# The last pass of a decode backward kernel: three engines in the written order, or in an order chosen at compile time with only the slab products kept in place

## The chip, the cores and the metric

The kernel runs on one core of one Trainium2 chip. The metric is device time in microseconds (us) of one execution; three executions of the kernel before are given, and their median is the number to compare with. One further record, the profile, shows when each instruction of one execution ran.

## The reference, cut to what matters

A decoder step for one token goes through attention, a dense layer, the same attention again and the same dense layer again, with the same weights and caches both times. The kernel computes the output and all gradients:

```
x = x + A(layernorm(x), k_cache, v_cache, wq, wo)   # 32 query heads, 4 groups, 65536 keys of 128
x = x + B(layernorm(x), w1, b1, w2, b2)             # squared relu, 3584 wide
x = x + A(layernorm(x), ...)
x = x + B(layernorm(x), ...)
out, vjp = jax.vjp(f, x, k_cache, v_cache, wq, wo, w1, b1, w2, b2);  grads = vjp(grad_out)
```

The gradients of the two caches are as large as the caches (67 MB each, bf16), and each is a sum over both attention layers of outer products, so that the last pass reads both caches and writes both gradients.

## The kernel before, in words

There are four passes over the caches: two forward passes, one backward pass for the upper attention layer, and a last pass (`attn_bwd4`) that does the backward of the lower layer and writes the cache gradients of both layers. Dense stages stand between them.

The last pass goes through 256 items, each of 8 columns of 128 keys, in four groups g; four items are a block (J = 32 columns). `pipeline` calls, for each step i, a list of stages, each with a lag in steps; a stage is a Python function that issues instructions for the item that is due:

- `vT` (L1313): loads the block of V when it is new, transposes 8 tiles on TensorE (L1321) into a PSUM tile `ps_tr`, and evicts it into a tile `kt` (four buffers).
- `vS` (L1341): 8 matmuls of `kt` with `DOB` into `ps_sc` (L1352, one buffer in this pass), once a block opened by a matmul at L1349; at the block's end VectorE multiplies with the kept exponentials into `X` (L1369).
- `eIn` (L1327): GpSimd copies a block of exponentials into `xin` (L1330, one buffer). `eT` (L1373) and `xT` (L1379): four transposes a block each (L1336) and an eviction into `xt`. `eT` also sets up small matrices (`su_setup`: L1296 on VectorE, L1301 on GpSimd, L1303 on TensorE, L1305 and L1307 on VectorE).
- `dV8` and `dK8` (`outer16`, L1384): the outer products that are the cache gradients. Each fills a 128x1024 PSUM tile `ps_gg` with a pair of 512-wide matmuls (L1392), which ScalarE or VectorE evicts into a staging slot (L161 and L164, the two lines of the helper `evac`); a full slot is stored from GpSimd's queue (L1398). There are 512 such pairs in the pass and two `ps_gg` buffers.
- `k8` (L1411): 8 matmuls of the K block with `X` into `ps_acc` (L1423).

Beside these, `bg.step` issues one piece of background work in a step: the outer products of the weight gradients (`rows2` L1455 and `rank2` L1470, which also use `ps_gg`), and the products of weight slabs with a vector (`g_rowdots`: VectorE multiplies a slab with the vector at L583, ScalarE sums it at L572). In this pass L583 is already followed by `tc.keep_in_program_order(ins)`, which puts the product behind the instruction of VectorE that was written before it.

The order of the work: the pass stands in `tc.manual_schedule(engines=ORDERED)`, where ORDERED is TensorE, VectorE and ScalarE. In these the instructions stay in the order in which the Python code issues them. SyncE (the loads, L350 for the caches and L447 for the weights) and GpSimd (copies, stores) are not in the set: the framework's list scheduler places their instructions at compile time, by its own estimate of when inputs and buffers are ready, and among ready ones by the written order. Each engine then runs its queue strictly in that order. Loads and stores use slots of one arena that the Python code hands out in the written order.

`evac` chooses between ScalarE and VectorE by running totals of estimated work, while the Python code runs. At the end of the pass, `fill4` (ten steps before the end) transposes the last weight slabs (L669), and after the pass the last gradient rows are computed and stored (L1491, L208).

Of the kernel before, what the change touches and what calls it, by code (L numbers as in the profile page):

```python
# [11 lines left out]
F32 = mybir.dt.float32  # L12
ACTF = mybir.ActivationFunctionType
ALU = mybir.AluOpType
AX = mybir.AxisListType
PSUM = bass.MemoryType.PSUM
P = 128
# [3 lines left out]
def kernel(  # L21
# [24 lines left out]
    nc = tc.nc  # L46
    D = A_x.shape[-1]
# [7 lines left out]
    DC, FC = D // P, F // P  # L55
# [10 lines left out]
    TLEAD = 2  # L66
# [9 lines left out]
    tmp = ctx.enter_context(tc.tile_pool(name="tmp", bufs=2))  # L76
# [23 lines left out]
    def ps_mv(shape, dtype=F32):  # L100
        if PS["pass4"]:
            return ps_tr(shape, dtype)
        return PS["pool"].tile(shape, dtype, name="ps_mv", tag="mv", bufs=1)
# [98 lines left out]
    def col_to_dram(col, n, v1d):  # L202
        nj = n // P
        pt = ps_mv([nj, P], F32)
        nc.tensor.transpose(pt[:, :], col[:, :], ident_f[:, :])
        rows = tmp.tile([nj, P], BF, name="rows_c", tag="rows_c")
        nc.vector.tensor_copy(out=rows[:], in_=pt[:])
        nc.gpsimd.dma_start(out=v1d.rearrange("(j p) -> j p", p=P), in_=rows[:])  # L208

    def bcast_sum(src, ncols, mean=False):  # L210
        pt = ps_mv([P, ncols], F32)
        nc.tensor.matmul(pt[:, :], lhsT=(onesd_f if mean else ones_f)[:, :], rhs=src, start=True, stop=True)
        return pt
# [23 lines left out]
    def ln_bwd(dn, n, rstd):  # L237
        st = tmp.tile([P, 2], F32, name="lnb_st")
        nc.vector.reduce_sum(out=st[:, 0:1], in_=dn, axis=AX.X)
        pr = tmp.tile([P, DC], F32, name="lnb_pr")  # L240
        nc.vector.tensor_tensor(out=pr[:], in0=dn, in1=n[:], op=ALU.mult)
        nc.vector.reduce_sum(out=st[:, 1:2], in_=pr[:], axis=AX.X)
        tot = bcast_sum(st[:], 2, mean=True)
        negm = tmp.tile([P, 2], F32, name="lnb_negm")
        nc.vector.tensor_scalar(out=negm[:], in0=tot[:], scalar1=-1.0, scalar2=None, op0=ALU.mult)
        t = tmp.tile([P, DC], F32, name="lnb_t")
        nc.vector.scalar_tensor_tensor(out=t[:], in0=n[:], scalar=negm[:, 1:2], in1=dn, op0=ALU.mult, op1=ALU.add)
        dx = tmp.tile([P, DC], F32, name="lnb_dx")
        nc.vector.tensor_scalar(out=dx[:], in0=t[:], scalar1=negm[:, 0:1], scalar2=rstd[:, 0:1], op0=ALU.add, op1=ALU.mult)
        return dx  # L250
# [20 lines left out]
    def hold(i):  # L271
        HELD.add(i)
        FREE.pop(i, None)
# [122 lines left out]
    DK_LAG = TLEAD + J // 8 + 1  # L396
    B4_LAG = DK_LAG + J // 8
    DV_LAG = TLEAD + 1
    V_LEAD = 4 * J // 8
    ITEMS = [order_by_unit(False, SU), order_by_unit(True, SU), order_by_unit(False, HB), order_by_unit(True, J)]  # L400
    V_SHIFT = lambda k: min(V_LEAD, max(0, (k - V_LEAD) // 3))
# [197 lines left out]
    class Rows:  # L599
# [147 lines left out]
        def run(self):  # L747
            self.fill()
            first = self.queue[0][0] if self.queue else None
            while first is not None and first["inplace"] and self.queue and self.queue[0][0] is first:  # L750
                self.back()
            self.fill()
            while self.queue:
                self.back()
                self.fill()
# [67 lines left out]
    def tasks(i):  # L823
        for fn in TASKS.pop(i, ()):
            fn()

    def pipeline(items, stages, bg, end=(), holds=(), lead=None):

        def due(lag):
            at = {}  # L830
            for k, it in enumerate(items):
                at.setdefault(k + lag + LEAD if lead is None or lag >= 0 else k + ~lag + lead(k), []).append(it)
            return at
        LEAD = 0 if lead is None else lead(len(items))
        when = [due(l) for _, l in stages]
        maxlag = max(l for _, l in stages) + LEAD
        for i in range(len(items) + maxlag):
            NOW["i"] = i
            NOW["wide"] = NOW["pairs"]
            for at, k in holds:  # L840
                if i == at:
                    hold(k)
            tasks(i - 0.5)
            for n, (fn, lag) in enumerate(stages):
                for it in when[n].get(i, ()):
                    fn(*it)
                if n == 0:
                    tasks(i)
            bg.step(max(0, i - LEAD))
            NOW["wide"] = False  # L850
            NOW["step"] += 1
            for before, fn in end:
                if i == len(items) + maxlag - before:
                    fn()
        while TASKS:
            k = min(TASKS)
            NOW["i"] = int(k + 0.5)
            tasks(k)


    def new_layer(name, lay):
        L = dict(name=name)
        for nm in ("qT", "oT", "rZ", "dOT", "dqT"):
            L[nm] = vec.tile([P, HQ], F32, name=name + "_" + nm)
        L["oTb"] = vec.tile([P, HQ], BF, name=name + "_oTb")
        L["qpad"] = vec.tile([P, G, 8, R], BF, name=name + "_qpad")
        L["negm"] = vec.tile([P, G, NSU, R], F32, name=name + "_negm")
        L["fw"] = vec.tile([P, G, NSU, R], F32, name=name + "_fw")
        L["nd2"] = vec.tile([64, HQ], BF, name=name + "_nd2")
        nc.gpsimd.memset(L["nd2"][:], 0.0)  # L870
        return L
# [22 lines left out]
    def gsl(g):  # L894
        return slice(g * R, (g + 1) * R)
# [81 lines left out]
    def g_dn(L, dn, g, first):  # L977
        yield from g_rowdots(wq_slabs(g)[0], DC, L["dqT"][:, gsl(g)], R, dn_finish(dn, first), "%s_dn%d" % (L["name"], g))
# [4 lines left out]
    ORDERED = {mybir.EngineType.PE, mybir.EngineType.DVE, mybir.EngineType.Activation}  # L983
# [281 lines left out]
    def attn_bwd4(p, La, Lb, on_group, bg, stack, end=()):  # L1265
        dspool = stack.enter_context(tc.tile_pool(name="b4_ds", bufs=2))
        items = ITEMS[p]
# [170 lines left out]
        for b in range(V_LEAD * 8 // J // 2):  # L1438
            nexts.append(("k",) + items[(b + 2) * J // 8])
            nexts.append(("v",) + items[(b + NKEEP[2]) * J // 8])  # L1440
        with tc.manual_schedule(engines=ORDERED):
            pipeline(items, [(eIn, 0), (dV8, DV_LAG), (dK8, DK_LAG), (xT, DK_LAG - 1), (vS, ~TLEAD), (eT, TLEAD), (vT, ~0), (k8, B4_LAG)], bg,
                     end, lead=V_SHIFT)

# [48 lines left out]
    def g_outer(pool, out_dram, nA, nB, a_cols, b_cols, c0=0, a_f=False):  # L1495

        rb = pool.tile([66, 4 * P], BF, name="rowb", tag="rowb")
        rows2(b_cols, (0, 4), rb)
        yield
        for a0 in range(0, nA, 4):  # L1500
            ra = pool.tile([66, 4 * P], BF, name="rowa", tag="rowa", bufs=2)
            rows2(a_cols, (a0, a0), ra)
            yield
            sl = Slot("og", True)
            og = sl.t[:, :].rearrange("p (j n) -> p j n", j=4)
            for j in range(4):
                rank2(og[:, j, :], lambda r: d_cols(ra[r, :], j) if a_f else f_cols(ra[r, :], j), lambda r: rb[r, :])
                if j < 3:
                    yield
            nc.gpsimd.dma_start(out=out_dram[a0 * P:(a0 + 4) * P, c0:c0 + 1024].rearrange("(p j) n -> p j n", j=4), in_=og)  # L1510
            sl.free(stored=True)
            yield
# [39 lines left out]
    L1, L3 = new_layer("L1", 0), new_layer("L3", 1)  # L1552
# [33 lines left out]
    PRE = {}  # L1586

    def pre_load(key, pair):
        def f():
            PRE[key] = prefetch(pair())  # L1590
        return f

    gxbc = bcast_vec(gx[:], DC)
    bg = Background()
# [17 lines left out]
    rows = Rows(DENSE["pool"])  # L1612
# [20 lines left out]
    bg = Background()  # L1633
# [14 lines left out]
    rows = Rows(DENSE["pool"])  # L1648
# [15 lines left out]
    bg = Background()  # L1664
# [15 lines left out]
    dx1 = vec.tile([P, DC], F32, name="dx1")  # L1680
# [12 lines left out]
    rows = Rows(DENSE["pool"])  # L1693
# [27 lines left out]
    bg = Background()  # L1721
# [6 lines left out]
    dn1 = vec.tile([P, DC], F32, name="dn1")  # L1728
# [13 lines left out]
    def gwq(g):  # L1742
        return g_outer(bgpool, out_4, DC, R, [L3["n"], L1["n"]], [L3["dqT"][:, gsl(g)], L1["dqT"][:, gsl(g)]], c0=g * 1024)

    def on4(g):
        if g != lastg[3]:
            bg.add(g_dn(L1, dn1, g, g == firstg[3]))
            bg.normal.append(gwq(g))

    def last_v():  # L1750

        for g, c8 in ITEMS[3][-3 * J // 8::J // 8]:
            kv8("v", g, c8)

    def fill4():
# [5 lines left out]
                                  lastg[3] * 1024)  # L1761
        next(PRE["gwq"])
    attn_bwd4(3, L1, L3, on4, bg, b4, [(12 + B4_LAG, last_v), (20, pre_load("wq4", lambda: wq_slabs(lastg[3], 2))), (10, fill4)])
    next(PRE["gwq"])
    PRE["rows"].run()
    next(PRE["gwq"])
    dxn1 = ln_bwd(dn1[:], L1["n"], L1["rstd"])
    dx0 = tmp.tile([P, DC], F32, name="dx0")
    nc.vector.tensor_tensor(out=dx0[:], in0=dx1[:], in1=dxn1[:], op=ALU.add)
    col_to_dram(dx0, D, out_1.rearrange("a b d -> (a b d)"))  # L1770
    run(PRE["gwq"])
    b4.close()
    ps4_stack.close()

# [29 lines left out]
```

## Time and profile before

| | |
|---|---|
| three runs | 2132.25, 2144.49 (median), 2154.23 us |
| profiled execution, its own time | 2144.49 us |
| its span, first to last instruction | 2142.7 us |
| mean granted TensorE clock | 0.852 of full speed |
| last pass, first matmul of `vS` to last of `k8` | 1212.7 to 2124.5 us |
| moved by DMA over the span | 794.98 MB |

The profiled execution is the median run; 1.8 us of its time lie outside the span. In the views below, PE is TensorE's matmuls, PEld its weight loads, DVE VectorE, ACT ScalarE, POOL GpSimd, SP SyncE (SPq its queue). A line of waits reads: engine, what waited and its line, the releaser, the total, the number of times, the longest.

### The profile page before, as it was taken

What the parts mean: (1) busy time and instruction counts of PE and PEld (TensorE: products, weight loads), DVE (VectorE), ACT (ScalarE), POOL (GpSimd) and SP (SyncE); (2) the same over time, 40 slices, a digit from 0 to 9 for tenths busy, and PEclk for the clock granted to TensorE, in tenths of its full rate; (3) what the DMA queues carried; (4) which work ended last, traced back from release to release, by engine and by line L of the source; (5) the groups of instructions that cost most, each with busy time, mean ns of one, the idle gap of its engine ahead of it and who ended that gap; (6) DMA issues with size and microseconds to landing.
All of it is one profiled execution on the core that took longest, in us unless ns stands there. A gap on an engine that the chain in (4) does not pass through costs nothing. (4 is left out here: it accounts for less than half of the span.)

```text
span 2142.7 us, 67169 instructions
## 1 busy us (share of the span) xinstructions
PE 1657.9 (77%) x30228; PEld 1348.5 (63%) x30228; DVE 1185.3 (55%) x2414; ACT 1047.8 (49%) x1620; POOL 141.7 (7%) x332
## 2 busy tenths in 40 slices
PE   7887776887788878788788777777676777787775
PEld 6877776787777767677778644444454545454443
DVE  5655553464555445354445556656477567656655
ACT  3434443354344534254443456546466556656654
POOL 0000000000000000000000011111011111111111
PEclk9989997899999979998999867758699779869877
DMA  9999999999999989999999769879799979999954
GB/s 393 421 424 420 425 424 391 389 422 423 420 424 424 406 307 367 421 423 412 424 416 361 263 236 375 351 291 368 287 388 387 395 284 405 386 350 370 360 231 177
DMA packets 101038, 794.98 MB, mean 371 GB/s; under 512 B 9472, under 2 KB 9486, under 8 KB 37134
## 3 DMA queue, kind: packets, MB, share of 16 engines
q1 hardware_dynamic: 76670, 624.99, 72.9%
q0 software_dynamic: 24080, 165.70, 18.9%
q8 instruction: 236, 3.87, 0.7%
q14 instruction: 52, 0.43, 0.1%
HBM read 624.96 MB, written 165.69 MB: 369 GB/s over the span
## 5 line engine op out<-in xcount | busy, mean ns | idle before, releaser
L164 DVE COPY kt<-ps_tr 128x1024 bf16<-128x1024 bf16 x715 | 491.2, 688 | 462.2 <-PE ps_tr L1009 252.2
L161 ACT CAST arena<-ps_gg 128x1024 bf16<-128x1024 f32 (+2 forms) x445 | 429.8, 1002 | 262.3 <-PE ps_gg L1470 142.1
L1009 PE MATMUL ps_tr<-ident_b,arena 128*128 128x128 bf16 x3840 | 313.7, 227 | 41.0 <-DMA arena<-in_A_k_cache_dram 28.4
L164 DVE CAST arena<-ps_gg 128x1024 bf16<-128x1024 f32 (+1 forms) x198 | 241.4, 1220 | 166.9 <-PE ps_gg L1392 150.4
L1392 PE MATMUL ps_gg<-GG,xt 64*128 64x512 bf16 x1024 | 227.1, 457 | 134.4 <-ACT arena L161 85.0
L161 ACT COPY kt<-ps_tr 128x1024 bf16<-128x1024 bf16 x173 | 180.5, 1048 | 201.9 <-PE ps_tr L1201 116.7
L1009 PEld LDWEIGHTS <-arena 128*128 128x128 bf16 x3840 | 236.9, 102 | 50.7 <-DMA arena<-in_A_k_cache_dram 32.1
L1111 PE MATMUL ps_acc<-arena 128*128 128x64 bf16 (+4 forms) x4096 | 207.9, 197 | 60.3 <-DMA arena<-in_A_v_cache_dram 48.9
L1392 PEld LDWEIGHTS <-xt 64*128 64x128 bf16 x1024 | 53.2, 97 | 251.6 <-issue 214.8
L1111 PEld LDWEIGHTS <-arena 128*128 128x128 bf16 x4096 | 161.5, 101 | 65.3 <-DMA arena<-in_A_v_cache_dram 52.5
L1092 ACT ACTIVATE arena<-S_sb,L_negm 128x128 bf16<-128x128 f32 x256 | 165.6, 1003 | 61.3 <-DVE L_negm L1077 61.2
L1027 PE MATMUL ps_sc<-L_qpad,kt 128*128 128x64 bf16 (+7 forms) x3584 | 185.1, 195 | 12.6 <-ACT kt L161 5.9
L1201 PE MATMUL ps_tr<-ident_b,arena 128*128 128x128 bf16 x1920 | 158.6, 230 | 43.2 <-DMA arena<-in_A_v_cache_dram 42.5
L1321 PE MATMUL ps_tr<-ident_b,arena 128*128 128x128 bf16 x1824 | 171.6, 250 | 14.3 <-DVE T L1305 4.9
L1027 PEld LDWEIGHTS <-kt 128*128 128x128 bf16 x3584 | 155.3, 101 | 16.8 <-ACT kt L161 8.3
L1201 PEld LDWEIGHTS <-arena 128*128 128x128 bf16 x1920 | 120.7, 103 | 47.7 <-DMA arena<-in_A_v_cache_dram 45.3
L1321 PEld LDWEIGHTS <-arena 128*128 128x128 bf16 x1824 | 135.1, 114 | 22.9 <-issue 22.9
L1352 PEld LDWEIGHTS <-kt 128*128 128x128 bf16 x1824 | 81.0, 108 | 90.3 <-issue 90.3
L1092 ACT ACTIVATION_READ_ACCUMULATOR arena<-S_sb,L_negm 128x1 f32 x256 | 127.9, 500 | 0.0
L1246 PE MATMUL ps_acc<-dsT,arena 128*128 128x64 bf16 (+7 forms) x2048 | 104.5, 196 | 11.9 <-DMA arena<-in_A_k_cache_dram 9.6
L572 ACT ACTIVATE mv_t<-mv_t 128x1024 bf16<-128x1024 bf16 x96 | 101.7, 1061 | 9.3 <-DVE mv_t L583 9.2
L1352 PE MATMUL ps_sc<-DOB,kt 128*128 128x64 bf16 (+3 forms) x1824 | 105.0, 207 | 0.0
(292 smaller groups left out, 2196.7 us busy)
## 6 DMA issues: line engine op xcount, KB each, us to landing
arena<-in_A_k_cache_dram SPq DMA_DIRECT2D x86, 2048.0 KB, 21.4
arena<-in_A_v_cache_dram SPq DMA_DIRECT2D x83, 2048.0 KB, 21.8
out_dram<-arena POOLq DMA_DIRECT2D x149, 1024.0 KB, 8.9
arena<-in_A_v_cache_dram SPq DMA_DIRECT2D x76, 1024.0 KB, 10.0
arena<-in_A_k_cache_dram SPq DMA_DIRECT2D x76, 1024.0 KB, 8.4
arena<-in_B_w_dram SPq DMA_DIRECT2D x32, 896.0 KB, 7.6
arena<-in_A_wo_dram SPq DMA_DIRECT2D x22, 1024.0 KB, 13.8
arena<-in_A_wq_dram SPq DMA_DIRECT2D x20, 1024.0 KB, 15.2
```

Of the source, the lines that this page charges most:

```text
L161: nc.scalar.copy(out=out, in_=in_)
L164: nc.vector.tensor_copy(out=out, in_=in_)
L572: nc.scalar.activation(out=t[:, :], in_=t[:, :], func=ACTF.Copy, accum_out=y[:, kc:kc + 1])
L1009: nc.tensor.transpose(pt[:, i, :], kb8[:, i, :], ident_b[:, :])
L1027: nc.tensor.matmul(state["ps_s"][:, s:s + w, :].rearrange("p a b -> p (a b)"), lhsT=kt[:, i, :], rhs=L["qpad"][:, g, 0:w, :].rearrange("p ...
L1092: nc.scalar.activation(out=E(p, g, c0, SU)[:, :, h], in_=S[:, h, :], func=ACTF.Exp, bias=L["negm"][:, g, su, h:h + 1], scale=SCALE, accum_ ...
L1111: nc.tensor.matmul(ps_o[:, 0:w, :], lhsT=vb8[:, i, :], rhs=E(p, g, c, w), start=(c % SU == 0), stop=(c % SU == SU - 1), skip_group_check=True)
L1201: nc.tensor.transpose(pt[:, i, :], vb8[:, i, :], ident_b[:, :])
L1246: nc.tensor.matmul(ps_dq[:, 0:w, :].rearrange("p a b -> p (a b)"), lhsT=kb8[:, i, :], rhs=dsT[:, s:s + w, :].rearrange("p a b -> p (a b)") ...
L1321: nc.tensor.transpose(pt[:, i, :], vb8[:, i, :], ident_b[:, :])
L1352: nc.tensor.matmul(state["ps_dp"][:, s:s + w, :].rearrange("p a b -> p (a b)"), lhsT=vt[:, i, :], rhs=DOB[:, g, 0:w, :].rearrange("p a b - ...
L1392: nc.tensor.matmul(pg[:, 512 * h:512 * h + 512], lhsT=xt[64 * h:64 * h + 64, j1 // 8 + m, :], rhs=gg[64 * h:64 * h + 64, :, :].rearrange(" ...
```

## The change

The `manual_schedule` around the last pass goes. The three engines' instructions are then placed as SyncE's and GpSimd's already are, and only the products at L583 stay behind what was written before them on VectorE. The stages are written in another order within a step: vT, vS, eIn, eT, dV8, xT, dK8, k8 in place of eIn, dV8, dK8, xT, vS, eT, vT, k8; their lags are the same. The code that ends the kernel (last weight gradient, last layernorm backward) moves from behind the call of `attn_bwd4` into `on4`, which the last `k8` of the last group calls; it is the last work of the pass, so its written order stays.

```
-        with tc.manual_schedule(engines=ORDERED):
-            pipeline(items, [(eIn, 0), (dV8, DV_LAG), (dK8, DK_LAG), (xT, DK_LAG - 1), (vS, ~TLEAD), (eT, TLEAD), (vT, ~0), (k8, B4_LAG)], bg,
-                     end, lead=V_SHIFT)
+        pipeline(items, [(vT, ~0), (vS, ~TLEAD), (eIn, 0), (eT, TLEAD), (dV8, DV_LAG), (xT, DK_LAG - 1), (dK8, DK_LAG), (k8, B4_LAG)], bg,
+                 end, lead=V_SHIFT)
...
         if g != lastg[3]:
             bg.add(g_dn(L1, dn1, g, g == firstg[3]))
             bg.normal.append(gwq(g))
+        else:
+            next(PRE["gwq"])
+            PRE["rows"].run()
+            next(PRE["gwq"])
+            dxn1 = ln_bwd(dn1[:], L1["n"], L1["rstd"])
+            dx0 = tmp.tile([P, DC], F32, name="dx0")
+            nc.vector.tensor_tensor(out=dx0[:], in0=dx1[:], in1=dxn1[:], op=ALU.add)
+            col_to_dram(dx0, D, out_1.rearrange("a b d -> (a b d)"))
+            run(PRE["gwq"])
...
     attn_bwd4(3, L1, L3, on4, bg, b4, ...)
-    next(PRE["gwq"])
-    PRE["rows"].run()
-    next(PRE["gwq"])
-    dxn1 = ln_bwd(dn1[:], L1["n"], L1["rstd"])
-    dx0 = tmp.tile([P, DC], F32, name="dx0")
-    nc.vector.tensor_tensor(out=dx0[:], in0=dx1[:], in1=dxn1[:], op=ALU.add)
-    col_to_dram(dx0, D, out_1.rearrange("a b d -> (a b d)"))
-    run(PRE["gwq"])
```

## The prediction

> **What bounds the kernel now.** I read the page's slices first, then the stretches of the last pass, then the waits of each queue in it, then one step of the timeline. The slices show where the change can act: the last pass fills slices 23 to 40, and there TensorE's clock and the DMA share both drop.
>
> ```profile
> PE   7887776887788878788788777777676777787775
> PEclk9989997899999979998999867758699779869877
> DMA  9999999999999989999999769879799979999954
> ```
>
> The next view cuts the pass into stretches. Columns: the stretch, its length, busy us of each engine with the number of instructions, granted clock, DMA share, GB/s.
>
> ```profile
> 1212.00:1262.00 50.00, 37.47 (x351) 20.08 (x352) 21.43 (x45) 19.90 (x23) 6.20 (x12) 0.52 0.56 201
> 1262.00:1505.00 243.00, 186.47 (x2070) 114.64 (x2070) 148.77 (x263) 138.56 (x163) 36.16 (x71) 0.72 0.88 340
> 1505.00:1755.00 250.00, 181.87 (x2264) 117.81 (x2264) 154.82 (x277) 144.58 (x175) 34.18 (x66) 0.79 0.91 353
> 1755.00:2000.00 245.00, 187.21 (x2398) 120.03 (x2396) 161.56 (x277) 155.13 (x190) 39.72 (x77) 0.84 0.96 373
> 2000.00:2125.00 125.00, 88.22 (x1101) 56.52 (x1098) 71.34 (x134) 67.76 (x76) 17.01 (x30) 0.82 0.64 247
> ```
>
> Summed over 913 us: TensorE 681 us (75%), VectorE 558 (61%), ScalarE 526 (58%), and DMA, weighted by length, 785 (86%). None is full. The pass takes 913/256 = 3.57 us an item. What holds it is read from the waits of TensorE, whose idle time is 913 - 681 = 232 us.
>
> ```profile
> PE ps_gg L1392 <- ACT arena L161: 85.0, 142, 1.3
> PE ps_gg L1455 <- DVE r_cc L1453: 37.0, 33, 2.8
> PE ps_tr L1303 <- POOL CC L1301: 20.1, 11, 3.0
> PE ps_gg L1392 <- ACT rowa L161: 15.4, 18, 1.1
> PE ps_sc L1349 <- DVE X L1369: 11.0, 6, 9.9
> PE ps_gg L1392 <- DVE xt L164: 10.9, 19, 1.1
> PE ps_gg L1392 <- DVE arena L164: 9.4, 15, 1.1
> ...
> PE ps_gg L1392 <- DVE rowa L164: 4.9, 6, 1.1
> ...
> PE ps_gg L1392 <- ACT rowb L161: 3.3, 4, 0.9
> ```
>
> The L1392 lines other than the one on xt are waits for a ps_gg buffer: 85.0 + 15.4 + 9.4 + 4.9 + 3.3 = 118.0 us in 185 waits, 0.64 us each, at 185 of 512 pairs (36%). No line names a load. Counting the n-th load of V against the n-th group of 32 transposes in the timeline, loads are issued 26 to 90 us before use and land in a median 8.5 us. So the transfers don't set the pace; the two ps_gg buffers with their evictions do. The step itself shows it: TensorE stands 0.78 us at its second pair, behind two ScalarE evictions in a row, while the eight-matmul groups behind it wait in line.
>
> ```profile
> 1700.72 1.93 ACT L161 CAST arena<-ps_gg 128x1024 bf16<-128x1024 f32 x2 [0.57 <-PE ps_gg L1470]
> ...
> 1701.78 0.39 PE L1392 MATMUL ps_gg<-GG,xt 64*128 64x512 bf16 x2 [0.78 <-ACT arena L161]
> ...
> 1702.11 0.38 PE L1352 MATMUL ps_sc<-DOB,kt 128*128 128x64 bf16 x8
> ...
> 1702.34 0.61 PE L1321 MATMUL ps_tr<-ident_b,arena 128*128 128x128 bf16 x8
> ```
>
> **The change part by part.** No instruction on a data path is added or taken away: the same matmuls, evictions, loads and stores. Only orders change, so every term is a difference of waits. The sum goes against the profiled execution, 2144.5 us (span 2142.7 and 1.8 around it), which is also the median of the three.
>
> Pairs at L1392. In the written order each pair has a fixed place, with 0.38 + 0.61 + 0.40 = 1.39 us an item of other TensorE work (L1352, L1321, L1423) standing as one stretch between them. In a free order these groups are taken as soon as the estimate calls them ready, and loads that land tens of microseconds early make them ready early; they are limited only by four kt buffers and one ps_sc. What has been taken early is missing as cover later, and the order is frozen while durations are not: a pair of 512-wide matmuls took 0.61 us at 1231 us and 0.39 at 1700, the clock being 0.52 and 0.79. Bounds: if all buffer waits go, -118.0; if each of the 512 pairs waits 0.64, 512 x 0.64 - 118 = +210. The nearest row is a queue of this same pass that is already placed freely, GpSimd's:
>
> ```profile
>   PE ps_tr L1336: 177.6, 40
> ```
>
> That is line L1330's idle time: 40 of the 64 xin copies (63%) stand at the head of their queue waiting for the buffer, with stores queued behind them. I take this share for the pairs: 0.63 x 512 = 323 waits x 0.64 = 207, less 118: +89 us. The row is of another engine, so both ends stay for the range.
>
> Waits for small set-up work: L1455 behind VectorE's casts (37.0) and L1303 behind GpSimd's (20.1), 57.1 us. Here the written order is at its worst, since a free one can put a ready group in front. Bounds 0 and -57.1; half: -29 us. If the cover for them is gone, they stay.
>
> Start of the pass. Until 1225.8 us ScalarE stands 16.4 us for the first piece of background work, which waits in the written order behind the first four blocks of vS. The weight-gradient products need nothing of these. Bounds 0 and -16.4; half: -8 us.
>
> Products at L583 keep their place: 48 of 0.68 us with no idle before them in the view of that line. Behind one wait VectorE's evictions and, through them, the pairs; the only row like it is VectorE's X behind a weight slab, 10.8 us, once. I take 0; bounds 0 and two such, +22. Their sums on ScalarE (1.06 us) may slide; what waits for them is needed a group (64 items) later.
>
> Moved stages, and the loads and stores that they issue. vT stands first in the step, so its loads are written before the step's stores. SyncE's queue waited 617.7 us for stores to give back slots; a shift of one step (3.57 us) is taken from a lead of at least 26, less 8.5 of landing. Cost 0; if the lead were gone, each of the 119 cache loads could cost up to 8.5 us, which bounds it only far off. GpSimd's queue keeps its kind of order, but its stores follow later evictions.
>
> The tail, moved into on4, is written in the same place; it took 2124.5 to 2142.7. Cost 0, bounds -5 and +5 (a store on GpSimd waits 5.2 us there).
>
> Clock. By the starts of k8's blocks, a block took 13.8 us from 1250 to 1498 us (clock 0.72) and 13.0 from 1755 to 2002 (0.84). A change of clock of that size is worth at most 0.8 us in 64 blocks, 51 us either way; which way, nothing shows: 0.
>
> Sum: 2144.5 + 89 - 29 - 8 = 2196.5, rounded 2197 us.
>
> A rule that speaks against an effect: after the rows above, the Trainium skill ("Perfetto Trace Analysis", Optimization Strategy) says that consistent bubbles can mean too few PSUM buffers for the next tile. By it the 0.64 us waits belong to the two ps_gg buffers, and no order alone would add or remove many: that sum would be 2144.5 - 29 - 8 = 2107.5. The trace agrees on the buffer and not on the constancy, as 64% of the pairs don't wait, so order matters here.
> A second rule: the skill's "TensorE: Matmul & The Clock Gate" (Part 1) puts the slow state after an idle window of about 3.4 us, so more waits of 0.64 us would leave the clock alone. The trace doesn't fit it here: from 1212 to 1262 us the clock is 0.52 with no TensorE wait over 1.5 us.
>
> **The rivals.** Faster: the free order puts the 1.39 us of independent work between the pairs. For it: inputs land early, TensorE idles 232 us, and DMA leaves 913 - 785 = 128. Against: two buffers, a frozen order. With half of the buffer waits gone as well: 2144.5 - 59 - 29 - 8 = 2048; a quarter: 2078. It decides if fewer than 185 pairs wait.
>
> No change: two ps_gg buffers, one ps_sc and four kt leave the free order so little room that the same rhythm comes out, and set-up waits return as pair waits. For it: each item must still make two pairs and two evictions. 2144.5, give or take 1%.
>
> Much slower: the lead of the loads is eaten. If the arena's slots come back later because stores wait behind xin copies and late evictions, TensorE stands in line for data with landed work behind. For it: SyncE already waits 617.7 us on stores. Against: a lead of 26 to 90 us. Priced with all pairs waiting, +210, and nothing gained: 2354; with 16 weight loads each late by 2.7 us beside the forecast: 2240. It sets in when a load's lead falls below 8.5 us.
>
> **How the numbers follow.** Forecast 0.60 (its own range 2150 to 2250), faster 0.12, no change 0.12, much slower 0.16. The range 2115 to 2300 leaves out about half of the faster case and half of the slowest one. A measurement of this kernel tells about 1% from no change (2123 to 2166). Faster by over 1%: 0.12. Within 1%: 0.12 and 0.08 of the forecast's low end, 0.20. Slower: 0.52 and 0.16, 0.68.
>
> **What would show it.** The pair step is right if TensorE's buffer waits at L1392 rise from 118 us towards 207 and their number from 185 towards 323; wrong if both fall. The set-up step is right if the waits at L1455 and L1303 fall from 57 towards 29. The start is right if ScalarE's 16.4 us shrink. The lead is untouched if no line of TensorE's waits names a load. The forecast is wrong above all if the eight-matmul groups end up between the pairs, or if VectorE or ScalarE, not TensorE, turn out to stand in line for something written later than they were placed.

## The result, and the profile after

The changed kernel took 2014.49 us (median of 4 runs, 2008.13 to 2018.73) against 2145.96 us (2132.25 to 2154.23): a ratio of 0.939, 95% interval [0.934, 0.945]. It is faster by 6%, where the forecast was slower by 2.4%. Its profiled execution took 2018.73 us, with a span of 2017.0 and a mean granted clock of 0.890.

The slices of the changed kernel, TensorE's matmuls, its granted clock and the DMA share:

```profile
PE   6878888687878787878788888878779888877897
PEclk9999899699999997899888999778889889976978
DMA  9999999999999998999999988999999999999997
```

The first half of the rows is nearly as before. In the last pass the DMA row, which stood at 6 to 9 with a 5 and 4 at the end, is now almost all nines. The same as sums over the last pass, first the kernel before, then the changed one (stretch, length, busy us and number of instructions of TensorE, its weight loads, VectorE, ScalarE, GpSimd, then clock, DMA share, GB/s):

```profile
1212.00:2125.00 913.00, 681.23 (x8179) 429.08 (x8179) 557.92 (x994) 525.93 (x624) 133.26 (x254) 0.77 0.86 332
```

```profile
1212.00:2001.00 789.00, 653.86 (x8172) 409.48 (x8173) 542.15 (x969) 521.27 (x608) 135.82 (x250) 0.85 0.96 384
```

The pass is 124 us shorter with the same work. TensorE's idle time (length less busy time) fell from 232 to 135 us. Its busy time, in which the profile models the ends of matmuls, fell by 27 us, at a clock of 0.85 in place of 0.77: that part of the gain is faster matmuls, not fewer waits. The DMA share rose from 0.86 to 0.96. TensorE's waits in the last pass of the changed kernel (engine, line, releaser, total us, times, longest; L1454 and L1469 are here what L1455 and L1470 are in the kernel before):

```profile
PE ps_tr L1321 <- DMA arena<-in_A_v_cache_dram: 45.3, 13, 8.4
PE ps_acc L1423 <- DMA arena<-in_A_k_cache_dram: 36.3, 12, 12.0
PE ps_sc L1349 <- DVE X L1369: 18.2, 3, 11.0
PE ps_gg L1392 <- ACT arena L161: 10.2, 22, 2.5
...
PE ps_gg L1469 <- ACT arena L161: 3.3, 10, 0.7
PE ps_gg L1392 <- DVE arena L164: 3.3, 5, 1.4
...
PE ps_gg L1392 <- DVE rowa L164: 0.8, 2, 0.5
...
PE ps_gg L1392 <- ACT rowa L161: 0.4, 2, 0.3
```

The buffer waits at L1392 are 10.2 + 3.3 + 0.8 + 0.4 = 14.7 us in 31 waits; before they were 118.0 in 185. The two set-up waits (L1455 and L1303, 57.1 us before) are gone; 0.9 us of other waits are left at L1454. In their place stands what the kernel before never had: 45.3 + 36.3 = 81.6 us of TensorE waiting for loads of the caches. The chain of work that ended last, as far as the profile follows it back, says the same (shares of the span; first before, where it holds no transfer, then changed):

```profile
PE 2%; ACT 1%; DVE 1%; issue 1%; POOL 0%; POOLq 0%; ACTq 0%; DVEq 0%
```

```profile
DMA 9%; PE 8%; ACT 3%; DVE 2%; issue 1%; POOL 0%; POOLq 0%; SPq 0%; DVEq 0%; ACTq 0%
```

What the new order does can be seen in TensorE's lines of the timeline. Before, a step's work stands in blocks; the second pair of L1392 waits:

```profile
1703.11 0.41 PE L1470 MATMUL ps_gg<-rowb,rowa 2*128 2x512 bf16 x2
1703.54 0.39 PE L1392 MATMUL ps_gg<-GG,xt 64*128 64x512 bf16 x2
1704.68 0.39 PE L1392 MATMUL ps_gg<-GG,xt 64*128 64x512 bf16 x2 [0.75 <-ACT arena L161]
```

After, the eight-matmul groups are broken up and laid between the pairs:

```profile
1608.40 0.61 PE L1392 MATMUL ps_gg<-GG,xt 64*128 64x512 bf16 x2
...
1608.94 0.22 PE L1423 MATMUL ps_acc<-X,arena 128*128 128x32 bf16 x2
...
1609.01 0.91 PE L1321 MATMUL ps_tr<-ident_b,arena 128*128 128x128 bf16 x7
...
1609.85 0.41 PE L1469 MATMUL ps_gg<-rowb,rowa 2*128 2x512 bf16 x2
...
1610.19 0.23 PE L1321 MATMUL ps_tr<-ident_b,arena 128*128 128x128 bf16 x1
```

Three ps_gg tiles in a row are three fillings on two buffers; the third stands until the first is evicted. In the trace before, 150 of 193 buffer waits at L1392 (103 of 120 us; 8 short ones behind the eviction at L557 are counted here too) are at the second pair after a background product (L1470, L1455 or L555) and a first pair.

### The profile page after: what moved, and what is told of

Same layout as the page of the kernel before. It is cut to its first block, busy times and chain, and to the rows that moved or that the text cites. A ratio compares the mean times of both kernels' runs of the same rounds, so it can differ in the third digit from the quotient of the medians.

```text
span 2017.0 us, 67084 instructions
## 1 busy us (share of the span) xinstructions
PE 1627.1 (81%) x30228; PEld 1325.1 (66%) x30228; DVE 1173.5 (58%) x2426; ACT 1045.6 (52%) x1608; POOL 145.4 (7%) x332
## 5 line engine op out<-in xcount | busy, mean ns | idle before, releaser
L161 ACT CAST arena<-ps_gg 128x1024 bf16<-128x1024 f32 x457 | 445.3, 1010 | 241.0 <-PE ps_gg L1392 172.2
L1009 PE MATMUL ps_tr<-ident_b,arena 128*128 128x128 bf16 x3840 | 312.1, 227 | 39.4 <-DMA arena<-in_A_k_cache_dram 26.9
L164 DVE CAST arena<-ps_gg 128x1024 bf16<-128x1024 f32 (+2 forms) x186 | 222.1, 1194 | 105.5 <-PE ps_gg L1392 72.5
L161 ACT COPY kt<-ps_tr 128x1024 bf16<-128x1024 bf16 x164 | 171.4, 1049 | 195.0 <-PE ps_tr L1201 111.9
L1009 PEld LDWEIGHTS <-arena 128*128 128x128 bf16 x3840 | 235.8, 102 | 48.9 <-DMA arena<-in_A_k_cache_dram 30.3
L1392 PE MATMUL ps_gg<-GG,xt 64*128 64x512 bf16 x1024 | 217.0, 427 | 21.1 <-ACT arena L161 10.2
L1321 PE MATMUL ps_tr<-ident_b,arena 128*128 128x128 bf16 x1824 | 181.4, 237 | 48.2 <-DMA arena<-in_A_v_cache_dram 45.3
L1111 PEld LDWEIGHTS <-arena 128*128 128x128 bf16 x4096 | 160.9, 101 | 66.5 <-DMA arena<-in_A_v_cache_dram 49.5
L1321 PEld LDWEIGHTS <-arena 128*128 128x128 bf16 x1824 | 121.3, 105 | 105.7 <-issue 55.3
L1201 PE MATMUL ps_tr<-ident_b,arena 128*128 128x128 bf16 x1920 | 157.6, 228 | 40.3 <-DMA arena<-in_A_v_cache_dram 37.0
L1201 PEld LDWEIGHTS <-arena 128*128 128x128 bf16 x1920 | 119.3, 102 | 46.2 <-DMA arena<-in_A_v_cache_dram 39.8
L1423 PEld LDWEIGHTS <-arena 128*128 128x128 bf16 x2048 | 94.7, 103 | 74.9 <-DMA arena<-in_A_k_cache_dram 38.3
L1352 PE MATMUL ps_sc<-DOB,kt 128*128 128x64 bf16 (+3 forms) x1824 | 118.7, 201 | 0.0
L1246 PE MATMUL ps_acc<-dsT,arena 128*128 128x64 bf16 (+7 forms) x2048 | 104.2, 195 | 14.7 <-DMA arena<-in_A_k_cache_dram 9.7
L1423 PE MATMUL ps_acc<-X,arena 128*128 128x64 bf16 (+3 forms) x1536 | 94.8, 199 | 22.8 <-DMA arena<-in_A_k_cache_dram 22.8
```

The lines of the kernel that those rows point to most:

```text
L161: nc.scalar.copy(out=out, in_=in_)
L164: nc.vector.tensor_copy(out=out, in_=in_)
L1009: nc.tensor.transpose(pt[:, i, :], kb8[:, i, :], ident_b[:, :])
L1111: nc.tensor.matmul(ps_o[:, 0:w, :], lhsT=vb8[:, i, :], rhs=E(p, g, c, w), start=(c % SU == 0), stop=(c % SU == SU - 1), skip_group_check=True)
L1201: nc.tensor.transpose(pt[:, i, :], vb8[:, i, :], ident_b[:, :])
L1246: nc.tensor.matmul(ps_dq[:, 0:w, :].rearrange("p a b -> p (a b)"), lhsT=kb8[:, i, :], rhs=dsT[:, s:s + w, :].rearrange("p a b -> p (a b)") ...
```

## Experiments

Theory O: the freedom of order is the cause, TensorE's above all. Theory S: the new order of stages is the cause. After the first four runs, theory R: the written order lost its time because background work and two pairs stand in a row; and theory D: the changed pass is held by its transfers. Times are medians of four executions beside seven of the kernel before on the same chip; each ratio is to those. A table below gives each run's last pass by stretch, with TensorE's idle and busy time and clock in it.

**Freedom alone** (e1): the kernel before without `manual_schedule`.

```
-        with tc.manual_schedule(engines=ORDERED):
-            pipeline(items, [(eIn, 0), (dV8, DV_LAG), ..., (k8, B4_LAG)], bg, ...)
+        pipeline(items, [(eIn, 0), (dV8, DV_LAG), ..., (k8, B4_LAG)], bg, ...)
```

> The kernel before with manual_schedule taken away and nothing else: its own order of stages, its tail behind the pass. Theory O (the freedom of order is the cause, above all TensorE's): 2010 to 2045 us, TensorE's buffer waits at L1392 fall from 118 us to under 40. Theory S (the new order of stages, with other slots and another split of the evictions, is the cause): 2120 to 2150 us, buffer waits over 90 us.

Measured: 2015.03 us, 0.941 [0.939, 0.943], the time of the changed kernel; the waits at L1392 for a buffer 15.2 + 7.0 + 1.1 + 0.7 = 24.0 us. Time and waits are as theory O had them. Freedom is enough; neither the new order of stages nor the moved tail is needed with it.

**The new order of stages, written** (e2): the changed kernel with `manual_schedule` put back.

```
+        with tc.manual_schedule(engines=ORDERED):
             pipeline(items, [(vT, ~0), (vS, ~TLEAD), (eIn, 0), (eT, TLEAD), (dV8, DV_LAG), ..., (k8, B4_LAG)], bg, ...)
```

> The changed kernel with manual_schedule on TensorE, VectorE and ScalarE put back around the pipeline: the new order of stages, written. Theory O: at least 2120 us, perhaps slower than before, since the lags were set with the other order of stages; waits at L1392 over 90 us. Theory S: 2010 to 2045 us.

Measured: 2050.25 us, 0.958 [0.955, 0.960]. Neither theory said this (theory S is missed by 5 us): the order of stages, with nothing free, brings 90 of the 125 us. In it a k8 group lies between a step's pairs and the background product, and vT and vS between that and the next pairs (timeline of TensorE in this run):

```profile
1609.56 1.03 PE L1392 MATMUL ps_gg<-GG,xt 64*128 64x512 bf16 x4
1610.52 0.61 PE L1423 MATMUL ps_acc<-X,arena 128*128 128x64 bf16 x8
1611.27 0.62 PE L1470 MATMUL ps_gg<-rowb,rowa 2*128 2x512 bf16 x2
1611.82 1.03 PE L1321 MATMUL ps_tr<-ident_b,arena 128*128 128x128 bf16 x8
1612.65 0.63 PE L1352 MATMUL ps_sc<-DOB,kt 128*128 128x64 bf16 x8
```

**One side free** (e3, e4): the changed kernel with TensorE alone written, and with VectorE and ScalarE alone written.

```
+        with tc.manual_schedule(engines={mybir.EngineType.PE}):                                      # e3
+        with tc.manual_schedule(engines={mybir.EngineType.DVE, mybir.EngineType.Activation}):        # e4
```

> The changed kernel with TensorE alone in the written order; VectorE and ScalarE free. Theory O with TensorE as the engine that matters: 2110 us or more, most of the gain lost, waits at L1392 over 80 us. Theory V (free evictions on VectorE and ScalarE carry the gain): under 2060 us.

> The changed kernel with VectorE and ScalarE in the written order; TensorE free. Theory O with TensorE as the engine that matters: 2010 to 2060 us, waits at L1392 under 50 us. Theory V: 2100 us or more.

Measured: TensorE written 2022.22 us, 0.945 [0.943, 0.947]; TensorE free 2061.46 us, 0.962 [0.960, 0.964]. By its time e3 falls to theory V, against theory O's naming of TensorE; but e2, with nothing free, is itself under V's 2060 us, so that this says little. e4 misses theory O by 1.5 us and theory V by 39. In time, freeing TensorE alone is worth nothing beside e2 (11 us slower). Its idle time did fall, by 24 us, and the same matmuls took 36 us more (table below).

**Three tiles in a row, put back** (e6): e2 with k8 first in the step.

```
-            pipeline(items, [(vT, ~0), (vS, ~TLEAD), ..., (dK8, DK_LAG), (k8, B4_LAG)], bg, ...)
+            pipeline(items, [(k8, B4_LAG), (vT, ~0), (vS, ~TLEAD), ..., (dK8, DK_LAG)], bg, ...)
```

> The run with the new order of stages written on three engines (2050 us), with one stage moved: k8 stands first in the step instead of last. The two pairs of a step and the background's product that follows them then fill three ps_gg tiles in a row, as in the kernel before, with k8, vT and vS in one stretch after them. Theory R (three tiles in a row on two buffers are what the written order lost): 2110 to 2150 us, TensorE's waits for ps_gg over 100 us. Rival G (it was some other consequence of the new order: slots, split of the evictions, earlier loads): 2040 to 2065 us.

Measured: 2079.47 us, 0.973 [0.970, 0.975]: 29 us given back, not 60 or more, and in neither theory's range of time. TensorE's waits for ps_gg are over 100 us as theory R had it, and they have moved to the tile that is now third:

```profile
PE ps_gg L1470 <- ACT arena L161: 68.3, 95, 1.8
...
PE ps_gg L1470 <- DVE arena L164: 10.6, 11, 1.3
PE ps_gg L1455 <- ACT arena L161: 9.0, 11, 0.9
...
PE ps_gg L1392 <- ACT arena L161: 7.7, 24, 0.5
```

So three in a row costs something: over the pass the waits for a ps_gg buffer rise from 67 us in e2 to 111. But the kernel before, with 121 us of them, is 59 us slower than e6. Of that, 29 us are TensorE's matmuls, at a clock of 0.77 against 0.82 (table below); the rest is in this and other waits. What else the old order of stages cost isn't in this one edit.

**The old order, with one thing between** (e7, e10): the kernel before, written, with vT moved to the front of the step; and with its stages untouched, but the background's piece issued in the middle of the step.

```
-            pipeline(items, [(eIn, 0), ..., (eT, TLEAD), (vT, ~0), (k8, B4_LAG)], bg, ...)              # e7
+            pipeline(items, [(vT, ~0), (eIn, 0), ..., (eT, TLEAD), (k8, B4_LAG)], bg, ...)
...
                 if n == 0:                                                                              # e10
                     tasks(i)
+                if n == 4 and lead is not None:
+                    bg.step(max(0, i - LEAD))
-            bg.step(max(0, i - LEAD))
+            if lead is None:
+                bg.step(max(0, i - LEAD))
```

> The kernel before, written order on three engines, with one stage moved: vT stands first in the step instead of seventh, so that its eight transposes lie between the background's product and the next two pairs. Theory R: most of the gain of the new order of stages, 2045 to 2085 us, buffer waits at L1392 under 60 us. Rival G: 2120 to 2150 us.

> The kernel before, written order on three engines and its own order of stages, with one thing moved: the background's piece of a step is issued after vS, between the pairs and the next pairs, instead of at the end of the step directly ahead of them. Theory R (what is lost is that background work and two pairs stand in a row, on two buffers and with ScalarE's work queued up): 2045 to 2085 us, TensorE's buffer waits at L1392 under 60 us. Rival G (the order of the stages themselves is what mattered): 2115 to 2145 us.

Measured: e7 2060.39 us, 0.963 [0.960, 0.967]; e10 2082.72 us, 0.975 [0.967, 0.983]. Both lie in theory R's ranges, e10 at the upper edge. Moving one stage brings 78 us; moving no stage, only the background's place, brings 48 (35 to 70 by the interval). In e10 (its lines are 3 further down) the buffer waits in the pass fall from 121 to 69 us, and the set-up waits are as before:

```profile
PE ps_gg L1458 <- DVE r_cc L1456: 31.4, 28, 2.4
PE ps_tr L1306 <- POOL CC L1304: 28.1, 13, 3.0
PE ps_gg L1473 <- ACT arena L161: 21.6, 52, 0.9
PE ps_gg L1395 <- DVE arena L164: 18.2, 24, 12.1
...
PE ps_gg L1395 <- ACT arena L161: 14.9, 35, 1.2
```

**The products' place** (e5): the changed kernel without the line that its title names.

```
-            if PS["pass4"]:
-                tc.keep_in_program_order(ins)
```

> The changed kernel without the line that keeps the slab products in their written place on VectorE. Theory K (the products' place is not where the change's gain comes from): 2005 to 2035 us, within 1% of the changed kernel. Rival (the kept place protects VectorE's queue from slabs that have not landed): 2040 us or more, with VectorE waits for a weight load of over 40 us where the changed kernel has 18.

Measured: 2012.16 us, 0.940 [0.932, 0.949], the changed kernel's time. One product waited 8.5 us for its slab, and nothing came of it. Keeping the products in their place isn't what the gain comes from.

**What holds the changed pass** (e8, e9, e12): half of the cache gradients' stores left out, in the changed kernel, in the kernel before and in e2.

```
-                nc.gpsimd.dma_start(out=out, in_=stg)
+                nc.gpsimd.dma_start(out=out[:, 0:J // 2, :], in_=stg[:, 0:J // 2, :])
```

> The changed kernel, with only the first half of each staging slot of the cache gradients stored (the second half of those gradients is left out; all is still computed). 67 MB of the last pass's 303 MB of transfers go. Theory D (the changed pass is now held by its transfers): faster than the changed kernel by 50 us or more, 1900 to 1965 us. Rival E (TensorE and the evictions still hold it): 1990 to 2015 us.

> The kernel before with the same half of the cache gradients' stores left out. Theory D with R (before, the buffer waits hold the pass, not the transfers): 2115 to 2145 us, a gain of under 25 us. Rival (transfers held the pass before too): 2040 to 2090 us.

> The run with the new order of stages written on three engines (2050 us), with only the first half of each staging slot of the cache gradients stored (the second half of those gradients is left out). Theory D (in the middle of the pass the transfers hold this kernel too, though its three engines keep the written order): 1950 to 2000 us, at least 50 us less, but less gained than the 102 us of the changed kernel, since the written order's own waits come up next. Rival (the written order's waits hold it): 2025 to 2055 us.

Measured: the changed kernel 1912.46 us, 0.894 [0.891, 0.897], 102 us less; e2's order 2028.46 us, 0.948 [0.944, 0.952], only 22 less, where theory D expected 50 or more: its rival, that the written order's waits hold it, is right for e2. The kernel before gives no ratio and decides nothing: one execution took 2098.94 us at a clock of 0.881 and three took 2134.52 to 2140.13 at 0.848 to 0.853. In the changed kernel the waits for loads fall to 23 us:

```profile
PE ps_acc L1423 <- DMA arena<-in_A_k_cache_dram: 19.0, 5, 6.1
...
PE ps_tr L1321 <- DMA arena<-in_A_v_cache_dram: 4.0, 2, 2.7
```

That is 59 us of the 63 by which TensorE's idle time in the pass falls. Another 48 us are the same matmuls at a clock of 0.95 in place of 0.85; whether the freer transfers brought that, no run tells.

**Nearly all stores left out** (e15, e16), to settle the kernel before: `J // 8` in place of `J // 2`.

> The kernel before, storing only the first eighth of each staging slot of the cache gradients (the other seven eighths of those gradients are left out). Theory R: the written order's waits stay, 2090 to 2140 us, a gain of under 50 us though 117 MB of transfers go. Rival (the transfers held it too): under 2050 us.

> The changed kernel, storing only the first eighth of each staging slot (the rest of those gradients is left out). Theory D: clearly under the 1912 us of half the stores only if the transfers held even that one; 1840 to 1915 us. The waits of TensorE for loads fall under 25 us.

Measured: before 2116.75 us, 0.986 [0.979, 0.992]; changed 1870.43 us, 0.873 [0.869, 0.877]. The kernel before gains 23 us (16 to 45 by the interval) though seven eighths of 134 MB of stores are gone, and its waits for a ps_gg buffer stay at 119 us: its engines held it. The changed kernel gains 144. With so few stores the two lie 246 us apart, and with all of them about half of that: the rest shows only with the transfers out of the way. In the profiled executions 158 us of the difference are idle time of TensorE and 100 are its matmuls, at a clock of 0.99 against 0.76.

**Which freedom lowers that limit** (e13, e14): e3 and e4 with half of the stores.

> The changed kernel with TensorE alone in the written order, and only the first half of each staging slot of the cache gradients stored (the second half of those gradients is left out), so that the engines show and not the transfers. With all stores it took 2022 us. Theory V (what the free order adds to the new order of stages is VectorE's and ScalarE's freedom): 1910 to 1945 us. Theory P (TensorE's freedom): 1985 to 2030 us, near the 2028 of all three written.

> The changed kernel with VectorE and ScalarE in the written order and TensorE free, with the same half of the stores left out. Theory V: 1990 to 2050 us. Theory P: 1910 to 1960 us.

Measured: TensorE written, the others free, 1977.72 us, 0.924 [0.919, 0.928]; TensorE free, the others written, 2026.45 us, 0.944 [0.938, 0.950]. Beside 2028 (all written) and 1912 (all free), freeing VectorE and ScalarE is worth 51 us, freeing TensorE alone 2, and both together 116. e14 lies in theory V's range, e13 in neither. The times alone mislead here, as the last pass of the four runs shows (e12, all written; e13; e14; e8, all free; columns as above):

```profile
1210.90:2000.10 789.20, 641.74 (x8139) 404.19 (x8139) 553.51 (x996) 522.02 (x611) 133.61 (x253) 0.86 0.82 300
```

```profile
1211.80:1962.40 750.60, 615.83 (x8138) 391.19 (x8139) 549.93 (x969) 521.59 (x611) 137.79 (x251) 0.90 0.85 315
```

```profile
1210.80:1996.70 785.90, 687.06 (x8177) 416.90 (x8178) 542.10 (x996) 521.72 (x611) 133.54 (x253) 0.82 0.82 301
```

```profile
1213.70:1891.10 677.40, 605.48 (x8178) 388.08 (x8177) 537.75 (x975) 518.78 (x610) 135.66 (x249) 0.95 0.92 349
```

TensorE's idle time is 147 us all written, 135 with VectorE and ScalarE free, 99 with TensorE free and 72 all free. So alone it is TensorE's freedom that takes away more of the waits, as theory P had it. But its matmuls took 45 us more with TensorE alone free (clock 0.82 against 0.86), and 26 us less with the other two free (0.90), and this turned the times round. Why these orders ran at different clocks stays open, and so does which freedom matters more.

**Slots held back longer** (e11): the changed kernel with `STORE_STEPS = 8` in place of 5.

> The changed kernel with the arena's slots taken as stored 8 steps after a store is issued instead of 5, so that loads are put less often into slots whose store has not landed (SyncE waited 587 us for that in the changed kernel, and TensorE 82 us for loads). Theory D (the pass is held by the transfers' rate): 2000 to 2025 us, no change. Rival (the loads' place behind late stores costs TensorE its 82 us): 1950 to 1995 us. Fewer slots at hand may also make it slower.

Measured: 2010.24 us, 0.940 [0.933, 0.948], no change, as theory D had it, though SyncE's wait for stores fell from 587.2 to 505.6 us. TensorE's waits for loads stay (75.7 us).

The last pass by stretch, in us, from the first matmul at L1349 to the 64th of the 1024 at L1392, from there to the 960th, and to the last; then TensorE's idle and busy time over the three together, and its mean granted clock (all counted in the traces of the profiled executions):

| kernel | start | middle | end | idle | busy | clock |
|---|---|---|---|---|---|---|
| before | 66 | 777 | 68 | 231 | 680 | 0.77 |
| changed | 45 | 700 | 44 | 135 | 653 | 0.85 |
| e1, before's stages, free | 45 | 692 | 45 | 132 | 650 | 0.85 |
| e2, new stages, written | 62 | 690 | 58 | 159 | 650 | 0.84 |
| e3, TensorE written | 55 | 676 | 52 | 166 | 618 | 0.88 |
| e4, TensorE free | 59 | 703 | 59 | 135 | 685 | 0.81 |
| e6, k8 first | 64 | 721 | 60 | 194 | 651 | 0.82 |
| e7, vT first | 66 | 700 | 57 | 178 | 645 | 0.84 |
| e10, background in the middle | 64 | 730 | 60 | 184 | 670 | 0.80 |
| e12, e2 with half the stores | 63 | 669 | 58 | 147 | 642 | 0.86 |
| e13, e3 with half the stores | 58 | 639 | 53 | 135 | 616 | 0.90 |
| e14, e4 with half the stores | 59 | 665 | 63 | 99 | 687 | 0.82 |
| e8, changed with half the stores | 43 | 592 | 43 | 72 | 605 | 0.95 |
| e15, before with an eighth | 65 | 754 | 76 | 203 | 693 | 0.76 |
| e16, changed with an eighth | 40 | 554 | 44 | 45 | 593 | 0.99 |

The change's 122 us here are 21 at the start, 77 in the middle and 24 at the end; 95 of them are idle time of TensorE, 26 its matmuls. In the middle the new order of stages does as well written (690) as free (700). With half of the stores it doesn't: 669 against 592. So the free order's lead there is hidden by the transfers, while the written order is held by its own waits. The limit of the transfers isn't a sharp one, as e3 took 676 us with all stores. At the start and the end the free order keeps its lead (17 and 14 us); that fixed stretches of written work stand there without others to fill in is a reading that no run tests.

## Why the prediction was wrong, point by point

- **What bounds the kernel: right.** The waits for the two ps_gg buffers and their evictions were the largest part of TensorE's idle time (121 of 231 us), and the transfers did not hold the pass (e15).
- **Pairs at L1392: the step that failed.** The forecast took +89 us, from the share of GpSimd's xin copies that wait at the head of their queue (63%). Measured: buffer waits there fell from 118 to 15 us, -103 (the 118 leaves out 8 waits behind L557, 2.5 us). The borrowed row says nothing of TensorE: in the changed kernel 33 of the 64 xin copies still wait for the transposes of the block ahead (81.7 us) while only 31 of 512 pairs wait for a buffer (6%). A queue with one buffer and little to do can wait because nothing else is due, so that its share of waits is no price for another engine; whether those waits cost anything was not tested. The reason given beside it, that cover taken early is missing later, was argued and not seen; the groups were cut up and spread. What was in the shown lines all along was the better guide: a wait of 0.78 us with 1.39 us of other work queued behind it. The rival that said this was given 0.12, and was itself priced too small (2048 to 2078), since it let at least half of the waits stand and gave the clock nothing.
- **Set-up waits: right in kind, sized at half.** Forecast -29; measured, the 57.1 us are gone. The free order has the casts for L1455 done early, the first of them (of gx) at 10.5 us, before at 1224.7.
- **Start: right in kind.** Forecast -8. ScalarE's 16.4 us before its first piece of background work became 2.8, and the start stretch is 21 us shorter.
- **Products: 0 was right** (e5).
- **Loads and their lead: wrong.** "The lead is untouched if no line of TensorE's waits names a load": two lines do, with 81.6 us. The pass got so fast that the transfers caught up (333 to 383 GB/s in the pass), which the forecast had only as a danger. It caps the gain; it doesn't undo it (e8): TensorE's waits for all else fell from 227 to 44 us, and the loads put 82 back. Matched in order in the trace before, the 57 loads of V were issued 21 to 74 us ahead of their transposes, not 26 to 90; they had landed in time all the same.
- **Clock: taken as 0, measured at about -27.** TensorE's busy time fell by that for the same matmuls as the clock went from 0.77 to 0.85, within the 51 us either way that the forecast allowed. What raised the clock, no run here tells.
- **Tail: small, as forecast.** From the last pair to the end 18 us, before 20.
- **The two rules.** "Perfetto Trace Analysis" of the Trainium skill (Optimization Strategy) says that consistent bubbles can mean too few buffers. Here the same two buffers had 118 us of waits in one order and 15 in another, so that the buffer names the place, and the order sets the size. "TensorE: Matmul & The Clock Gate" (Part 1) lets the clock fall after idle windows of about 3.4 us. The traces here go the other way: the changed pass has 11 TensorE waits of over 3.4 us, up to 12.0, and a mean clock of 0.85, the pass before a single one and 0.77.

Of the forecast's sum, 2144.5 + 89 - 29 - 8, the term of the pairs was of the wrong sign, and with it the whole change.

## What to carry to other kernels

Where an engine waits at the head of its queue while ready work stands behind it, price a free order as a gain first, and take a loss only from a queue of the same engine. In an order written by hand, look for users of one small buffer pool that stand side by side across the step's border, background work among them: moving one independent group between them brought 78 of 125 us here (53 us less idle time in the pass, and 34 of faster matmuls). Ask how far the next limit is: here the transfers held the better of two quite different orders, so that they ended within 2% of each other. And compare idle and busy time of an engine before calling a freedom worthless: in e14 TensorE's idle time fell by 49 us and the matmuls took 45 more, so that the time alone showed nothing.

## What the runs showed of the hardware

- The same matmuls of one pass kept TensorE busy for 593 us at a mean granted clock of 0.99 (e16) and for 693 us at 0.76 (e15), on one chip, with the same bytes moved and in different orders.
- The clock does not go with the idle time. With the same bytes on the same chip, e13 had 135 us of TensorE idle in the pass and a clock of 0.90, e14 99 us and 0.82. The executions of each agree: over the whole run, the four of e13 had 0.912 to 0.922 and the four of e14 0.873 to 0.888; e3 and e4, with all stores, 0.894 to 0.911 and 0.867 to 0.872. What sets the clock stays open.
